# Window attention with a softplus feed-forward: one head's attention weights scaled on ScalarE, the other's on VectorE

## Chip, core and metric

The kernel runs on one core of a Trainium2 chip. The metric is the device time of one execution in microseconds (us). One execution is taken with a hardware profiler; times of the others come from runs without it. Engines: PE is TensorE (PEld its weight loads), DVE is VectorE, ACT is ScalarE, POOL is GpSimd, SP issues the transfers.

## What is computed

Eight batches of eight heads, 576 positions of 64 values. Each position attends to itself and the 63 before it; the result of all heads (4608 tokens of 512 values) goes through a feed-forward network of width 2048 with a softplus between its two products.

```python
scores = scale * np.matmul(q, k.transpose(0, 1, 3, 2))
mask = (rel >= 0) & (rel < window)          # rel = row - column, window = 64
scores = np.where(mask, scores, -1000000000.0)
attn = np.exp(scores - np.max(scores, axis=-1, keepdims=True))
attn = attn / (np.sum(attn, axis=-1, keepdims=True) + 1e-09)
out = np.matmul(attn, v)
...
h = x @ w_in
g = np.maximum(h, 0.0) + np.log1p(np.exp(-np.abs(h)))
return (g @ w_out).astype(np.float32)
```

## The kernel before

The tokens are cut into 12 blocks of 384 (`TB`), each of three tiles of 128 rows (`NJ`). For each block, `attention(g, hp)` runs four times, once for each pair of heads (`hp`), and the feed-forward runs 16 steps, one for each slice of 128 of the inner width. A step has `ffn_up` (12 products L450 into `ps_h`, then the softplus: absolute value L454, exponential L455 and logarithm L456 on ScalarE, the sum L458 on VectorE, and the split of the result in a high and a low part `g`, L460 and L461) and `ffn_down` (nine products L471 into `ps_o`). Products of full precision are made of three products of split operands. The order on TensorE puts the down-projection of a step behind the up-projection of the next.

One attention group has, for each of its three tiles j and for both heads `hh`: scores (L331 or L334), mask and minimum on VectorE (L342), the exponential with row sums on ScalarE (L345), then the sum plus 1e-9 (L352), its reciprocal (L353), and the scaling of the weights `p_t` by that reciprocal (L358), in place in SBUF. `p_t[0]` holds the first head, `p_t[1]` the second. Then each head's weights are transposed by TensorE (L379, L380), copied out of PSUM (L383, or L385 and L386), multiplied with the values (L416 or L427) and joined into `x` (L421, L422, or L431, L432 and L139, L140). For the first two blocks (`by_pe`) q and k are transposed by TensorE, and the scaling comes once behind all three tiles: six instructions in a row. For the others they are transposed by transfers (`tr<-nat`), and the scaling comes tile by tile.

In the opening, some 200 us, the kernel also loads the weights: 32 pieces of 512 KB of 64-bit numbers arrive by SP's queue (L156) and are put together into 32-bit numbers by `float64_split`: ScalarE (L161), GpSimd or VectorE (L162), VectorE (L163 to L165), ScalarE (L166) and GpSimd (L167).

The work is written as a list of events with due times (`BASE`, `PACE`, `STG`). A scheduler orders the instructions of each engine from it; TensorE's own order is kept as written from due time 100 on (`PE_ORDERED_FROM`). Each engine runs its instructions strictly in its order, and an instruction that waits holds all behind it.

Of the kernel before, what the change touches and what calls it, by code (L numbers as in the profile page):

```python
# [12 lines left out]
AF = mybir.ActivationFunctionType  # L13
ALU = mybir.AluOpType
# [22 lines left out]
def window_attention_softplus_ffn(  # L37
# [16 lines left out]
    nc = tc.nc  # L54
# [178 lines left out]
    def attention(g, hp):  # L233
# [6 lines left out]
        def bank():  # L240
            if not odd0:
                return ps_a.tile([P, 512], F32, name="ps_a")

            taken_ps[0] += 1
            return ps_o.tile([P, 512], F32, name=f"ps_o{taken_ps[0] % NJ}")
# [76 lines left out]
        rs = att.tile([P, NJ, 2], F32, name="rs", bufs=2)  # L322
        for j in range(NJ):
            first = j == 0 and not prev
            c0 = WIN if first else 0
            n = W - c0
            sp = bank()
            spv = sp[:, : 2 * n].rearrange("p (h c) -> p h c", h=2)
            kc = slice(j * P + WIN + c0, (j + 2) * P)
            if by_pe:  # L330
                mm(spv, qt[:, j * P : (j + 1) * P], kbd[:, :, j * P + c0 : j * P + W], start=True, stop=True)  # L331
            for hh in range(0 if by_pe else 2):
                for i, (a, b) in enumerate(((0, 0), (0, 1), (1, 0))):
                    mm(  # L334
                        spv[:, hh, :], tr_q[a][:, hh, j * P : (j + 1) * P], tr_k[b][:, hh, kc],
                        start=(hh == 0 and i == 0), stop=(hh == 1 and i == 2), skip_group_check=True,
                    )
            t = ORDER[g] * NJ + j
            m = mask_b if (t * P) % S + P > S else mask
            for hh in range(2):  # L340
                pv = p_t[hh][:, j, WIN + c0 :]
                nc.vector.tensor_tensor_reduce(  # L342
                    pv, spv[:, hh, :], m[:, c0:], 1.0, 3.0e38, ALU.add, ALU.min, mn[:, j, hh : hh + 1]
                )
                nc.scalar.activation(  # L345
                    pv, pv, AF.Exp, bias=mn[:, j, hh : hh + 1], scale=-1.0, accum_out=sm[:, j, hh : hh + 1]
                )
            if by_pe and j < NJ - 1:
                yield
                continue  # L350
            jr = slice(0, NJ) if by_pe else slice(j, j + 1)
            nc.vector.tensor_scalar(rs[:, jr, :], sm[:, jr, :], 1.0e-9, None, ALU.add)  # L352
            nc.vector.reciprocal(rs[:, jr, :], rs[:, jr, :])  # L353
            for jj in range(jr.start, jr.stop):
                for hh in range(2):
                    c0 = WIN if jj == 0 and not prev else 0
                    pv = p_t[hh][:, jj, WIN + c0 :]
                    nc.vector.tensor_scalar(pv, pv, rs[:, jj, hh : hh + 1], None, ALU.mult)  # L358
            yield


# [142 lines left out]
    for g in range(NB):  # L504
        for hp in range(NP):
            if g < 3:
                base = BASE[g] + PACE[g] * hp
            else:
                base = 2 * NF * (g - 1) + SHP * hp + SH
            stages = attention(g, hp)  # L510
            for at in STG if g >= 3 else STG2 if g >= 2 else STG0:
                events.append((base + at, lambda stages=stages: next(stages, None)))
# [44 lines left out]
```

## Time and profile before

| | |
|---|---|
| median of 3 runs | 1071.59 us (1070.12 to 1072.89) |
| the profiled execution | 1069.74 us, span 1067.9 us |
| busy: PE, PEld | 1028.4 us (96%), 924.3 us (87%) |
| busy: DVE, ACT, POOL | 789.0 us (74%), 650.0 us (61%), 224.7 us (21%) |
| scaling L358 | 288 instructions, 110.4 us |
| exponential L345 | 288 instructions, 127.0 us |

The span runs from the first to the last instruction. Busy shares are over the whole span, and say little of a stage with another limit; so the rows below are mostly of stretches of time. Where an engine is said to have been idle "<- X", X is the instruction whose end let it go on.

### The profile page before, as it was taken

How to read it: one execution, taken by the hardware profiler on the slowest of the kernel's cores; microseconds unless marked ns; L12 is line 12 of the kernel's file. 1: busy time of each engine (PE TensorE's matmuls, PEld its weight loads, DVE VectorE, ACT ScalarE, POOL GpSimd, SP SyncE). 2: the span in 40 equal slices, each digit the busy share in tenths (PEclk: the TensorE clock that was granted, in tenths of full speed). 3: DMA queues.
4: the chain of work that ended last, by engine and by line, in shares of the span. 5: the costliest groups of instructions: out<-in, count | busy, mean ns of one | idle time of the engine just before them, and what ended most of it. 6: DMA issues, size and time to landing. Idle time of an engine off the chain costs nothing.

```text
span 1067.9 us, 18172 instructions
## 1 busy us (share of the span) xinstructions
PE 1028.4 (96%) x6096; PEld 924.3 (87%) x6096; DVE 789.0 (74%) x2319; ACT 650.0 (61%) x1669; POOL 224.7 (21%) x217
## 2 busy tenths in 40 slices
PE   7797988999999999999999999999999999999998
PEld 5576867888999899999999999999999999999996
DVE  4999899866777777777777777777777777865433
ACT  6786666666665666566656666656666665655333
POOL 4354355631111111112111111111211111110000
PEclk9999998999999999999999999999999999999999
DMA  7754645255334434343344334424434533520000
GB/s 197 198 140 105 169 105 146 67 127 119 70 71 101 96 79 105 64 97 81 81 96 96 84 76 93 107 60 88 102 74 84 115 80 62 131 51 1 30 1 30
DMA packets 296222, 98.20 MB, mean 92 GB/s; under 512 B 280512, under 2 KB 288704, under 8 KB 296128
## 3 DMA queue, kind: packets, MB, share of 16 engines
q1 hardware_dynamic: 296128, 97.03, 40.0%
q8 instruction: 48, 0.79, 0.3%
q14 instruction: 46, 0.38, 0.1%
HBM read 50.07 MB, written 10.22 MB: 56 GB/s over the span
## 4 chain that ended last, share of the span: by engine, by line
PE 78%; DVE 12%; DMA 4%; ACT 3%; issue 2%; SPq 1%; POOL 0%; DVEq 0%; ACTq 0%
PE ps_h L450 32%; PE ps_o L471 31%; PE ps_a L334 5%; PE ps_a L427 4%; PE ps_a L380 2%; DMA tr<-nat 2%; PE ps_a L379 2%; DVE p_t L358 2%; DVE osb L165 2%; DVE osb L164 1%; DVE osb L162 1%; DVE p_t L342 1%; DVE osb L163 1%; SPq L198 1%; DVE u L458 1%
## 5 line engine op out<-in xcount | busy, mean ns | idle before, releaser
L450 PE MATMUL ps_h<-x,w 128*128 128x384 f32 x2304 | 458.4, 344 | 15.4 <-DVE u L458 11.8
L471 PE MATMUL ps_o<-w,g 128*128 128x512 f32 x1728 | 438.7, 397 | 6.3 <-ACT g L460 4.3
L450 PEld LDWEIGHTS ps_h<-x,w 128*128 128x128 f32 x2304 | 400.6, 189 | 27.5 <-DVE u L458 12.5
L471 PEld LDWEIGHTS ps_o<-w,g 128*128 128x128 f32 x1728 | 318.1, 188 | 65.6 <-ACT g L460 4.6
L458 DVE SCALAR_TENSOR_TENSOR u<-ps_h,u 128x384 f32<-128x384 f32 x192 | 106.0, 552 | 139.7 <-ACT u L456 139.5
L454 ACT ACTIVATE u<-ps_h 128x384 f32<-128x384 f32 x192 | 93.6, 488 | 179.4 <-PE ps_h L450 177.2
L345 ACT ACTIVATE p_t<-p_t,mn 128x192 f32<-128x192 f32 (+1 forms) x288 | 127.0, 443 | 63.5 <-DVE mn L342 63.2
L140 POOL TENSOR_TENSOR x<-xf,x 128x384 fp32r<-128x384 f32 x40 | 41.1, 1027 | 460.6 <-DVE rs L352 362.9
L358 DVE TENSOR_SCALAR p_t<-p_t,rs 128x192 f32<-128x192 f32 (+1 forms) x288 | 110.4, 429 | 2.9
L342 DVE CUSTOM_DVE_ANT_0 p_t<-ps_a,mask 128x192 f32<-128x192 f32 (+1 forms) x244 | 77.3, 343 | 46.5 <-PE ps_a L334 36.1
L455 ACT ACTIVATE u<-u 128x384 f32<-128x384 f32 x192 | 100.7, 526 | 4.1
L456 ACT ACTIVATE u<-u 128x384 f32<-128x384 f32 x192 | 100.6, 524 | 3.2
L461 DVE TENSOR_TENSOR g<-u,g 128x384 fp32r<-128x384 f32 x160 | 89.5, 559 | 3.8 <-DVE g L460 0.5
L385 ACT CAST pt<-ps_a 128x512 fp32r<-128x512 f32 (+1 forms) x144 | 59.0, 417 | 33.7 <-PE ps_a L380 21.9
L312 POOL TENSOR_TENSOR nat<-q_in,nat 128x384 bf16<-128x384 f32 x40 | 38.6, 965 | 187.8 <-ACT nat L311 152.1
L386 DVE TENSOR_TENSOR pt<-ps_a,pt 128x512 fp32r<-128x512 f32 (+1 forms) x144 | 67.9, 477 | 12.3 <-ACT pt L385 10.7
L334 PE MATMUL ps_a<-tr 128*128 128x192 bf16 (+1 forms) x720 | 74.8, 246 | 0.9 <-DVE xf L432 0.7
L460 DVE CAST g<-u 128x384 fp32r<-128x384 f32 x176 | 67.9, 386 | 5.9
L380 PE MATMUL ps_a<-ident,p_t 128*128 128x128 f32 x276 | 66.6, 276 | 1.4 <-DVE p_t L358 1.3
L427 PEld LDWEIGHTS ps_a<-pt,vt 128*128 128x128 f32 (+1 forms) x608 | 64.0, 163 | 3.9 <-issue 0.5
L427 PE MATMUL ps_a<-pt,vt 128*128 128x64 f32 (+4 forms) x608 | 64.5, 247 | 0.4 <-DVE mn L342 0.4
L431 ACT COPY xf<-ps_a 64x384 f32<-64x384 f32 x80 | 38.1, 477 | 40.3 <-PE ps_a L427 37.5
(91 smaller groups left out, 1019.3 us busy)
## 6 DMA issues: line engine op xcount, KB each, us to landing
out_dram<-raw SPq DMA_DIRECT2D x12, 512.0 KB, 3.2
q_in<-in_q_dram SPq DMA_DIRECT2D x56, 96.0 KB, 2.6
raw<-in_moe_w_in_dram SPq DMA_DIRECT2D x10, 512.0 KB, 4.2
raw<-in_moe_w_out_dram SPq DMA_DIRECT2D x10, 512.0 KB, 4.2
k_in<-in_k_dram SPq DMA_DIRECT2D x32, 128.0 KB, 3.5
v_in<-in_v_dram SPq DMA_DIRECT2D x32, 128.0 KB, 2.8
raws<-in_moe_w_in_dram SPq DMA_DIRECT2D x6, 512.0 KB, 4.2
raws<-in_moe_w_out_dram SPq DMA_DIRECT2D x6, 512.0 KB, 5.0
```

Source lines behind the costliest of these rows:

```text
L334: mm(spv[:, hh, :], tr_q[a][:, hh, j * P : (j + 1) * P], tr_k[b][:, hh, kc], start=(hh == 0 and i == 0), stop=(hh == 1 and i == 2), skip_g ...
L342: nc.vector.tensor_tensor_reduce(pv, spv[:, hh, :], m[:, c0:], 1.0, 3.0e38, ALU.add, ALU.min, mn[:, j, hh : hh + 1])
L345: nc.scalar.activation(pv, pv, AF.Exp, bias=mn[:, j, hh : hh + 1], scale=-1.0, accum_out=sm[:, j, hh : hh + 1])
L358: nc.vector.tensor_scalar(pv, pv, rs[:, jj, hh : hh + 1], None, ALU.mult)
L427: mm(av[: D if lo else P, osl], vt[:, vb, hh, : 1 if lo else 2, :], pt[hh][lo][:, psl], start=(i == 0), stop=(i == len(order) - 1), skip_g ...
L450: mm(hv, weight(0, a, f)[:, c * P : (c + 1) * P], x[b][c], start=(i_mm == 0), stop=(i_mm == 3 * NC - 1))
L454: nc.scalar.activation(u, hv, AF.Abs)
L455: nc.scalar.activation(u, u, AF.Exp, scale=-1.0)
L456: nc.scalar.activation(u, u, AF.Ln, bias=1.0)
L458: nc.vector.scalar_tensor_tensor(gf, hv, 0.0, u, ALU.max, ALU.add)
L461: (nc.vector if g >= 2 else nc.gpsimd).tensor_tensor(gt[1], gf, gt[0].bitcast(F32), ALU.subtract)
L471: mm(ops[g][j], gt[a][:, js], weight(1, b, f), start=(first and i == 0), stop=(last and i == 2),)
```

## The change

Of the two heads of a group, the first is scaled on VectorE as before, the second by an ACTIVATE (Copy, with the reciprocal as a per-partition scale) on ScalarE. That moves 144 of the 288 instructions. Lines behind it have numbers higher by 3: the scaling on VectorE is L361, that on ScalarE L359, the reciprocal still L353, and the softplus L457, L458, L459 (ScalarE) and L461 (VectorE).

```diff
                 for hh in range(2):
                     c0 = WIN if jj == 0 and not prev else 0
                     pv = p_t[hh][:, jj, WIN + c0 :]
-                    nc.vector.tensor_scalar(pv, pv, rs[:, jj, hh : hh + 1], None, ALU.mult)
+                    if hh:
+                        nc.scalar.activation(pv, pv, AF.Copy, scale=rs[:, jj, hh : hh + 1])
+                    else:
+                        nc.vector.tensor_scalar(pv, pv, rs[:, jj, hh : hh + 1], None, ALU.mult)
             yield
```

VectorE's order, in the opening, at the first group of the second block (the run of six that starts at 47.85 us in the trace of before); `p_t_101` is the first head, `p_t_102` the second, `osb` a weight piece on its way. Before:

```order
L352 TENSOR_SCALAR rs<-sm 128x6
L164 SCALAR_TENSOR_TENSOR osb<-raws,osb 128x512
L353 RECIPROCAL rs<-rs 128x6
L165 SCALAR_TENSOR_TENSOR osb<-raws,osb 128x512
L358 TENSOR_SCALAR p_t_101<-p_t_101,rs 128x128
L358 TENSOR_SCALAR p_t_102<-p_t_102,rs 128x128
L358 TENSOR_SCALAR p_t_101<-p_t_101,rs 128x192
L358 TENSOR_SCALAR p_t_102<-p_t_102,rs 128x192
```

And now:

```order
L352 TENSOR_SCALAR rs<-sm 128x6
L165 SCALAR_TENSOR_TENSOR osb<-raws,osb 128x512
L353 RECIPROCAL rs<-rs 128x6
L425 TENSOR_TENSOR x_3_0_407<-ps_o_408,x_3_0_406 128x384
L361 TENSOR_SCALAR p_t_101<-p_t_101,rs 128x128
L361 TENSOR_SCALAR p_t_101<-p_t_101,rs 128x192 x2
L162 TENSOR_SCALAR osb<-osb 128x512
```

Three scalings stand there instead of six, and the next weight step follows at once; the join of `x` (L422, now L425), which stood behind the six, comes ahead of the three.

ScalarE's order for the same group, from its last two exponentials to the first softplus steps. Before:

```order
L345 ACTIVATE p_t_102,sm<-p_t_102,mn 128x192
L293 COPY kbd_114<-ps_a 64x384 x2
L166 CAST w_109<-osb 128x512
L421 CAST x_3_0_406<-ps_o_408 128x384
L282 ACTIVATE qpt<-ps_a 128x384
L166 CAST w_111<-osb 128x512
L161 ACTIVATE osb<-raw 128x512
```

And now:

```order
L345 ACTIVATE p_t_102,sm<-p_t_102,mn 128x192
L424 CAST x_3_0_406<-ps_o_408 128x384
L282 ACTIVATE qpt<-ps_a 128x384
L293 COPY kbd_114<-ps_a 64x384 x2
L161 ACTIVATE osb<-raw 128x512
L166 CAST w_111<-osb 128x512
L359 ACTIVATE p_t_102<-p_t_102,rs 128x128
L359 ACTIVATE p_t_102<-p_t_102,rs 128x192 x2
L457 ACTIVATE u<-ps_h 128x384 x2
```

The three scalings of the second head stand behind the weight cast and ahead of the softplus.

ScalarE's order in the long stretch behind the opening, at the third tile of an attention group (30 of the 40 groups behind the third block look like this). Before:

```order
L345 ACTIVATE p_t_101,sm<-p_t_101,mn 128x192
L345 ACTIVATE p_t_102,sm<-p_t_102,mn 128x192
L454 ACTIVATE u<-ps_h 128x384
L455 ACTIVATE u<-u 128x384
L456 ACTIVATE u<-u 128x384
L385 CAST pt_5289<-ps_a 128x64
```

And now:

```order
L345 ACTIVATE p_t_101,sm<-p_t_101,mn 128x192
L345 ACTIVATE p_t_102,sm<-p_t_102,mn 128x192
L457 ACTIVATE u<-ps_h 128x384
L458 ACTIVATE u<-u 128x384
L359 ACTIVATE p_t_102<-p_t_102,rs 128x192
L459 ACTIVATE u<-u 128x384
L388 CAST pt_5289<-ps_a 128x64
```

The scaling came in between the exponential and the logarithm of a feed-forward step. The scalings of the other two tiles stand ahead of the absolute value of the step before.

## Rows read from the trace of the kernel before

**Rows 1.** Busy time by engine in stretches, start:end, length, then granted clock.

```profile
core 0: us, PE busy (x) PEld busy (x) DVE busy (x) ACT busy (x) POOL busy (x), PEclk, DMA share, GB/s
25.00:205.00 180.00, 154.48 (x821) 129.21 (x819) 171.39 (x406) 121.89 (x309) 88.73 (x68) 0.96 0.53 138
300.00:1000.00 700.00, 699.33 (x4312) 642.36 (x4311) 516.05 (x1612) 427.89 (x1110) 101.08 (x104) 1.00 0.39 83
...
25.00:100.00 75.00, 61.46 (x311) 48.77 (x309) 74.10 (x189) 57.62 (x157) 34.17 (x27) 0.96 0.61 160
100.00:150.00 50.00, 44.84 (x260) 38.91 (x260) 44.84 (x98) 31.40 (x75) 23.38 (x19) 1.00 0.39 108
150.00:205.00 55.00, 48.18 (x254) 41.52 (x252) 52.45 (x121) 32.88 (x78) 31.18 (x24) 0.94 0.54 136
...
8.00:22.00 14.00, 11.13 (x54) 7.73 (x54) 8.64 (x44) 10.04 (x34) 2.46 (x5) 1.00 0.88 247
```

**Rows 2.** The same by stretches, of the scaling L358 alone (VectorE).

```profile
25.00:100.00 75.00, 15.39 (x32) 0.96 0.61 160
100.00:150.00 50.00, 5.75 (x12) 1.00 0.39 108
150.00:205.00 55.00, 8.05 (x14) 0.94 0.54 136
```

**Rows 3.** Groups, 25 to 205 us: count | busy us, mean ns | idle before, releasers.

```profile
L450 PE MATMUL ps_h<-x,w 128*128 128x384 f32 x300 | 66.4, 359 | 14.6 <-DVE u L458 11.1 <-ACT x L421 2.3 <-POOL w L167 0.9
...
L358 DVE TENSOR_SCALAR p_t<-p_t,rs 128x192 f32<-128x192 f32 (+1 forms) x56 | 29.2, 577 | 0.2
```

**Rows 4.** Order of time, VectorE then GpSimd: start, length, instructions [idle before].

```profile
14.71 1.40 DVE L358 TENSOR_SCALAR p_t<-p_t,rs 128x128 f32<-128x128 f32 x6
...
47.85 3.44 DVE L358 TENSOR_SCALAR p_t<-p_t,rs 128x128 f32<-128x128 f32 x6
...
19.80 1.49 POOL L162 TENSOR_SCALAR osb<-osb 128x512 f32<-128x512 f32 x1 [10.70 <-ACT osb L161]
...
47.77 2.71 POOL L167 TENSOR_TENSOR w<-osb,w 128x512 fp32r<-128x512 f32 x2 [6.09 <-ACT w L166]
```

**Rows 5.** Order of time at 59 us: last exponential of a group, then its reciprocal.

```profile
58.81 0.46 ACT L345 ACTIVATE p_t<-p_t,mn 128x192 f32<-128x192 f32 x1
59.16 0.20 ACT L345 ACTIVATION_READ_ACCUMULATOR p_t<-p_t,mn 128x1 f32 x1
...
60.29 0.19 DVE L353 RECIPROCAL rs<-rs 128x6 f32<-128x6 f32 x1
```

**Rows 6.** Order of time at 598 us: ScalarE, VectorE, TensorE.

```profile
598.75 0.53 ACT L455 ACTIVATE u<-u 128x384 f32<-128x384 f32 x1
599.31 0.53 ACT L456 ACTIVATE u<-u 128x384 f32<-128x384 f32 x1
...
598.60 0.17 DVE L353 RECIPROCAL rs<-rs 128x2 f32<-128x2 f32 x1
...
601.03 0.56 DVE L461 TENSOR_TENSOR g<-u,g 128x384 fp32r<-128x384 f32 x1
...
602.71 2.23 PE L471 MATMUL ps_o<-w,g 128*128 128x512 f32 x9
```

**Rows 7.** Order of time at 497 us: ScalarE, VectorE, TensorE.

```profile
497.06 0.53 ACT L455 ACTIVATE u<-u 128x384 f32<-128x384 f32 x1
...
497.27 0.17 DVE L353 RECIPROCAL rs<-rs 128x2 f32<-128x2 f32 x1
...
499.73 0.55 DVE L461 TENSOR_TENSOR g<-u,g 128x384 fp32r<-128x384 f32 x1
...
500.38 2.25 PE L471 MATMUL ps_o<-w,g 128*128 128x512 f32 x9
```

## The prediction

> **What bounds the kernel now.** I read the stretches first, since a share over the whole span mixes stages with different limits. From 300 to 1000 us TensorE is busy 699.33 of 700 us at a granted clock of 1.00 (its 2.4 GHz level), while VectorE and ScalarE have idle time [rows 1]. There the end moves only if TensorE is made to wait. From 25 to 205 us it is different: VectorE is busy 171.39 of 180 us, TensorE 154.48, ScalarE 121.89, GpSimd 88.73 [rows 1]. So TensorE has 25.5 us of holes in the opening, and the row of the up-projection's products says who makes them: of 14.6 us of idle before them, 11.1 ended with VectorE's softplus sum (L458) [rows 3]. That sum waits its turn in VectorE's queue among the weight splits and the attention weights' scaling. Broken down, VectorE is busy 74.10 of 75 us from 25 to 100, 44.84 of 50 from 100 to 150, and 52.45 of 55 from 150 to 205 [rows 1]: no gaps worth the name in the first and last of these, 5.2 us of gaps in the middle one. My reading is that the opening is paced by VectorE's queue, and that from about 205 us on the time is TensorE's work. What the change is worth is how much sooner the opening ends.
>
> **What leaves VectorE.** Half of the 288 scalings, one head of two. In the opening the row shows 56 of them with 29.2 us, a mean of 0.577 us; by stretches 32, 12 and 14 (two are counted at a border) with 15.39, 5.75 and 8.05 us [rows 2, 3]. Half is 28: 16 + 6 + 6 after rounding. What one is worth on the queue lies between two rows. With GpSimd quiet, six of them take 1.40 us from start to end, 0.23 each [rows 4]. At 47.85 us six take 3.44 us, 0.57 each, and two GpSimd subtractions run from 47.77 for 2.71 us beside them [rows 4]. So the long ones are long because of GpSimd. Taken out, one saves at least 0.23 us, 28 x 0.23 = 6.4 us, and at most its mean, 28 x 0.52 = 14.6 us (29.2 / 2). Which it is depends on whether the blocked time goes with the instruction or passes to its neighbour in the queue. GpSimd's 88.73 us of work are the same in both kernels. In the contended run, 2.0 us of delay (3.44 - 1.40) met 2.71 us of GpSimd: with three instructions instead of six, part of the delay would fall on the step behind, which is often another slow one, part on a step that isn't slowed. I take 0.35 us, nearer to the quiet row, since the queue behind is full: 28 x 0.35 = 9.8 us.
>
> A rule speaks for the lower end. The Trainium skill, SBUF — State Buffer, in its part on the two sides of the memory, says that VectorE's two-port instructions and GpSimd share a port pair as an exclusive lock for a whole instruction, and ScalarE has its own ports. That agrees with the two rows on the runs of six; by it the wait passes to the next two-port instruction, and the sum would be made with 0.23. That result is the first rival below.
>
> **What of it reaches the end.** In the two stretches without gaps, 22 instructions leave: 22 x 0.35 = 7.7 us. In the middle one VectorE already waits 5.2 us for others, so I count its 6 at nothing; counted fully they would add 2.1. The weight splits, the scalings that stay and the softplus sums stand in about the same mix in the new order, so the same work is pulled forward and no long step goes in ahead of it.
>
> **What comes onto ScalarE.** 144 scalings of 128x192 (some of 128x128). The trace has no plain scaling of that size there; the nearest is the exponential of the same tile with a per-partition operand: 0.46 us, and its accumulator read starts 0.35 us after it [rows 5]. So 0.35 to 0.46 us each: bounds for 28 of them are 9.8 and 12.9 us, onto an engine that has 58 us of idle time in the opening. Covered by that idle time, it costs nothing; if the cover is gone it costs those 9.8 to 12.9 us. Less than nothing it can't be: ScalarE drops no work. The first 25 us are the exception: between 8 and 22 us ScalarE is busy 10.04 of 14 us and VectorE 8.64 [rows 1], so neither has a full queue, and the chain runs from one to the other. Six scalings come to ScalarE there, ahead of the second pair's exponentials, and six quiet ones of 0.23 leave VectorE: between -1.4 (all the VectorE time is saved, ScalarE hidden) and +2.1 us (6 x 0.35, nothing saved). I take +1.2, two thirds of the way up, since the exponentials that follow in ScalarE's queue gate the next scaling. Sum: -7.7 + 1.2 = -6.5 us. The lower bound of the gain is 22 x 0.23 - 2.1 = 3.0 us, the upper 14.6 + 1.4 = 16.0.
>
> **The new wait.** The scaling on ScalarE waits for VectorE's reciprocal, and stands at the head of an in-order queue. Behind it stand, in the opening, the weight casts (L166), the absolute values (L161) and the first softplus steps; TensorE and GpSimd wait for those. In the stretch bound by TensorE, the order shows for 30 of the 40 attention groups the third scaling between the softplus's exponential and its logarithm. At 598 us that reciprocal ends at 598.77, the exponential at 599.28: the scaling finds its operand ready and pushes the logarithm from 599.31 by about 0.35 us. The split of g (L461) would end 0.35 later than 601.59, and TensorE starts the down-projection at 602.71 [rows 6]. So this is covered by 1.1 us of slack. In five groups the scaling stands ahead of the exponential. At 497 us the reciprocal ends at 497.44, the exponential had begun at 497.06: a push of some 0.75 us. There L461 ends at 500.28 and TensorE starts at 500.38 [rows 7]; its low part is read by the third product, two products later (2 x 0.23 us, nine taking 2.1), so such a place can cost 0.2 us. Two such places: under 0.5 us, left out of the sum. The transposes of the second head come a step after those of the first, so they are not hit.
>
> The Trainium skill, ScalarE: Activation LUTs, section Rules for kernel authors, says to put multiplications on VectorE and not on ScalarE. Per instruction this case's rows agree (0.23 us quiet against an estimated 0.35 to 0.46); the sum, made on the queue that is full, goes the other way, and by the rule alone the opening would lose 28 x 0.12 = 3.4 us.
>
> **Rivals.** (1) The blocked time stays: each removed scaling saves only the quiet 0.23, so 22 x 0.23 = 5.1, less 1.2, gives -3.9 us. For it: GpSimd's work doesn't change. Against: many VectorE steps in between read from TensorE's results and are not seen to slow down. (2) The relief is hidden anyway: the weights' transfers or ScalarE become the pace of the opening as soon as VectorE is quicker, and the end stays within 2 us either way. For it: the 5.2 us of gaps in the middle. Against: the queue that is full over 130 of 180 us. (3) Slower: ScalarE's queue is held at the new scalings. At 60 us the last exponential's read ends at 59.36 and the reciprocal at 60.48 [rows 5], 1.1 us. The opening has 18 such groups (five of three, thirteen single). Each held 1.1 us, with 28 x 0.35 of work, makes 30 us on ScalarE. It has 58 idle, but these are not where the holds fall; if about half, 16 us, lies on the path, the result is 16 - 9.8 = +6 us. It decides from the point where more than a third of the 30 us isn't covered. Against it: in the new order one to five other instructions stand between the exponentials and the scaling, which run in that time. (4) Slower in the long stretch: the scaling costs some 1.5 us instead of 0.4, or the reciprocal comes late, and 40 places each lose 0.3 us past the slack: +12 - 6.5 = +5.5 us. Against: 1.1 us of slack in the row.
>
> **How the numbers follow.** The profiled execution took 1069.74 us, 1.84 more than its span of 1067.9; the median of the runs is 1071.59, 1.85 above that execution. With -6.5: 1063.2 for an execution like the profiled one, 1065.1 for the median. Rivals in the median: (1) 1067.7, (2) 1071.6, (3) 1077.6, (4) 1077.1. Chances: the forecast 0.50, (1) 0.18, (2) 0.16, (3) 0.12, (4) 0.04. A measurement of this kernel tells about 0.3%, 3.2 us, from no change. The forecast and two thirds of (1) lie beyond that: 0.62 faster; (2) and the rest of (1): 0.22; slower 0.16. The range runs from the forecast's upper bound of the gain, 1071.6 - 16.0 = 1055.6, to 1073.5, which takes in nearly all of (2) and leaves out (3) and (4).
>
> **What would show it.** In the profile after: VectorE's busy time from 25 to 205 us down by 8 to 14 us; the last weight split (L165) and the first gapless stretch of TensorE earlier by some 6 us, and the same distance kept up to the end; TensorE's idle time before the up-projection less than 14.6 us; 144 scalings on ScalarE of 0.40 to 0.46 us each, some 60 us in all. 300 to 1000 us should stay gapless on TensorE. If the remaining scalings average over 0.6 us in the opening and the other VectorE steps grow, rival (1) holds. If ScalarE's idle time before L359 is long, and TensorE's waits name ScalarE (L166, L421 and its followers) instead of L458, it is (3). The prediction is wrong as a whole if the opening ends no earlier although VectorE's busy time fell, or if waits of TensorE appear after 300 us.

## The result, and the profile after

The changed kernel takes 1073.24 us (median of 20 runs, 1070.83 to 1075.73); the kernel before in the same comparison 1071.41 (20 runs, 1068.98 to 1072.89). The ratio is 1.0019, with a 95% interval of 1.0011 to 1.0027: some 2 us slower, less than the 0.3% that the prediction named as telling a change from none. The forecast was 1065.1. The time lies inside the forecast's range (1055.6 to 1073.5), but at its slow end, which was put there for rival 2. The profiled execution took 1072.42 us, its span 1070.6 (before 1067.9).

From the page of the profile, busy time by engine, then the two scalings (idle before, releaser):

```profile
PE 1029.3 (96%) x6096; PEld 928.6 (87%) x6096; DVE 756.2 (71%) x2175; ACT 702.4 (66%) x1813; POOL 224.9 (21%) x217
...
L359 ACT ACTIVATE p_t<-p_t,rs 128x192 f32<-128x192 f32 (+1 forms) x144 | 62.3, 444 | 27.5 <-DVE rs L353 24.3
...
L361 DVE TENSOR_SCALAR p_t<-p_t,rs 128x192 f32<-128x192 f32 (+1 forms) x144 | 67.3, 477 | 3.0
```

The edit does what it says: VectorE has 33 us less over the span, ScalarE 52 more. The stretches of [rows 1], now:

```profile
core 0: us, PE busy (x) PEld busy (x) DVE busy (x) ACT busy (x) POOL busy (x), PEclk, DMA share, GB/s
25.00:205.00 180.00, 153.66 (x810) 131.72 (x809) 165.84 (x380) 132.14 (x340) 88.96 (x68) 0.94 0.53 138
300.00:1000.00 700.00, 699.54 (x4308) 641.55 (x4307) 493.55 (x1519) 465.76 (x1216) 101.12 (x104) 1.00 0.39 82
25.00:100.00 75.00, 62.15 (x322) 51.96 (x320) 72.27 (x176) 63.79 (x174) 35.45 (x27) 0.95 0.60 158
100.00:150.00 50.00, 43.14 (x238) 37.58 (x239) 41.84 (x97) 32.01 (x80) 24.90 (x18) 0.97 0.42 118
150.00:205.00 55.00, 48.38 (x252) 42.19 (x251) 51.73 (x110) 36.34 (x88) 28.62 (x23) 0.91 0.52 127
```

The long stretch is as gapless as before: 699.54 of 700 us on TensorE. The opening isn't shorter: from 25 to 205 us VectorE's busy time fell by 5.5 us, and TensorE shows 11 matmuls and 0.8 us of busy time less than before. The products of the up-projection, the row of [rows 3] from 25 to 205 us:

```profile
L453 PE MATMUL ps_h<-x,w 128*128 128x384 f32 x294 | 68.3, 372 | 13.5 <-DVE u L461 8.6 <-DVE x L425 3.5 <-ACT x L424 1.4
```

The wait for the softplus sum shrank from 11.1 to 8.6, and a wait for VectorE's join of `x` (L425) took its place. So VectorE was relieved, and TensorE got nothing of it. The prediction's own sign of being wrong as a whole stands here: VectorE's busy time fell, and the opening ends no earlier. One place shows how. VectorE from 49 to 57 us in the changed kernel, in order of time: start, length, instruction; behind it ScalarE's two logarithms, whose results the two sums L461 wait for:

```profile
49.10 0.42 DVE L162 TENSOR_SCALAR osb<-osb 128x512 f32<-128x512 f32 x1
49.55 0.43 DVE L163 TENSOR_SCALAR osb<-osb 128x512 uint32<-128x512 uint32 x1
50.01 0.69 DVE L164 SCALAR_TENSOR_TENSOR osb<-raw,osb 128x512 uint32<-128x512 uint32 x1
...
51.55 0.69 DVE L165 SCALAR_TENSOR_TENSOR osb<-raw,osb 128x512 uint32<-128x512 uint32 x1
...
52.75 0.42 DVE L162 TENSOR_SCALAR osb<-osb 128x512 f32<-128x512 f32 x1
53.20 0.43 DVE L163 TENSOR_SCALAR osb<-osb 128x512 uint32<-128x512 uint32 x1
53.66 1.81 DVE L164 SCALAR_TENSOR_TENSOR osb<-raw,osb 128x512 uint32<-128x512 uint32 x1
55.40 0.34 DVE L342 CUSTOM_DVE_ANT_0 p_t<-ps_a,mask 128x192 f32<-128x192 f32 x1
...
55.95 0.68 DVE L165 SCALAR_TENSOR_TENSOR osb<-raw,osb 128x512 uint32<-128x512 uint32 x1
56.55 0.54 DVE L461 SCALAR_TENSOR_TENSOR u<-ps_h,u 128x384 f32<-128x384 f32 x1
...
53.45 0.95 ACT L459 ACTIVATE u<-u 128x384 f32<-128x384 f32 x2
```

Both logarithms are done at 54.40; the first sum starts at 56.55. Two whole weight pieces (L162 to L165) stand ahead of it, the last steps of them ahead of minima that ScalarE waits for (L342 at 55.40, behind a step that took 1.81 us where its like at 50.01 took 0.69). The first and the third sum in the kernel before, then the third in the changed one:

```profile
56.40 0.55 DVE L458 SCALAR_TENSOR_TENSOR u<-ps_h,u 128x384 f32<-128x384 f32 x1
...
67.61 0.55 DVE L458 SCALAR_TENSOR_TENSOR u<-ps_h,u 128x384 f32<-128x384 f32 x1
...
70.90 0.54 DVE L461 SCALAR_TENSOR_TENSOR u<-ps_h,u 128x384 f32<-128x384 f32 x1
```

So the first sum gained nothing, the third came 3.3 us late, and the last one of the kernel 2.67 us. The last weight split (L165) starts earlier, at 198.60 against 200.98, others up to 8.6 us earlier. The time that VectorE gained went to weight pieces, not to feed-forward steps.

### The profile page after: what moved, and what is told of

Same layout as the page of the kernel before. It is cut to its first block, busy times and chain, and to the rows that moved or that the text cites. A ratio compares the mean times of both kernels' runs of the same rounds, so it can differ in the third digit from the quotient of the medians.

```text
span 1070.6 us, 18257 instructions
## 1 busy us (share of the span) xinstructions
PE 1029.3 (96%) x6096; PEld 928.6 (87%) x6096; DVE 756.2 (71%) x2175; ACT 702.4 (66%) x1813; POOL 224.9 (21%) x217
## 4 chain that ended last, share of the span: by engine, by line
PE 81%; DVE 9%; DMA 3%; ACT 3%; issue 2%; SPq 1%; POOL 1%; DVEq 0%; ACTq 0%; POOLq 0%
PE ps_h L453 33%; PE ps_o L474 33%; PE ps_a L334 5%; PE ps_a L430 4%; PE ps_a L383 2%; PE ps_a L382 2%; DMA tr<-nat 2%; DVE osb L164 1%; DVE osb L165 1%; DMA raw<-in_moe_w_in_dram 1%; DVE u L461 1%; DVE p_t L342 1%; DVE osb L163 1%; DVE osb L162 1%; ACT p_t L345 1%
## 5 line engine op out<-in xcount | busy, mean ns | idle before, releaser
L461 DVE SCALAR_TENSOR_TENSOR u<-ps_h,u 128x384 f32<-128x384 f32 x192 | 106.4, 554 | 170.5 <-ACT u L459 170.3
L457 ACT ACTIVATE u<-ps_h 128x384 f32<-128x384 f32 x192 | 93.6, 488 | 124.1 <-PE ps_h L453 122.8
L342 DVE CUSTOM_DVE_ANT_0 p_t<-ps_a,mask 128x192 f32<-128x192 f32 (+1 forms) x244 | 77.3, 344 | 44.6 <-PE ps_a L334 33.8
L458 ACT ACTIVATE u<-u 128x384 f32<-128x384 f32 x192 | 100.8, 525 | 3.8
L459 ACT ACTIVATE u<-u 128x384 f32<-128x384 f32 x192 | 99.9, 521 | 2.1
L464 DVE TENSOR_TENSOR g<-u,g 128x384 fp32r<-128x384 f32 x160 | 90.4, 565 | 3.9 <-DVE g L463 0.5
L359 ACT ACTIVATE p_t<-p_t,rs 128x192 f32<-128x192 f32 (+1 forms) x144 | 62.3, 444 | 27.5 <-DVE rs L353 24.3
L334 PE MATMUL ps_a<-tr 128*128 128x192 bf16 (+1 forms) x720 | 74.3, 246 | 1.3 <-DVE pt L389 1.2
L361 DVE TENSOR_SCALAR p_t<-p_t,rs 128x192 f32<-128x192 f32 (+1 forms) x144 | 67.3, 477 | 3.0
```

The lines of the kernel that those rows point to most:

```text
L334: mm(spv[:, hh, :], tr_q[a][:, hh, j * P : (j + 1) * P], tr_k[b][:, hh, kc], start=(hh == 0 and i == 0), stop=(hh == 1 and i == 2), skip_g ...
L342: nc.vector.tensor_tensor_reduce(pv, spv[:, hh, :], m[:, c0:], 1.0, 3.0e38, ALU.add, ALU.min, mn[:, j, hh : hh + 1])
L457: nc.scalar.activation(u, hv, AF.Abs)
L458: nc.scalar.activation(u, u, AF.Exp, scale=-1.0)
L459: nc.scalar.activation(u, u, AF.Ln, bias=1.0)
L461: nc.vector.scalar_tensor_tensor(gf, hv, 0.0, u, ALU.max, ALU.add)
```

## Experiments

Two things had changed at once: the engine of 144 instructions, and the order that the scheduler made of everything else (of some 6,700 TensorE instructions 475 stood elsewhere, of VectorE's 190). To part them, the first two kernels hold each engine to a given order: a table of instruction numbers, and an order-only dependency from each to the one before it in the table, with no semaphore and no wait. A moved scaling gets the place in the program that its counterpart had.

```diff
+def lock_order(tc):
...
+    for n in seq:
+        i = here.get(f"I-{n}")
...
+        if e in last:
+            tc.add_manual_dep(
+                i, last[e], mybir.DependencyInfo(mybir.DependencyClass.NoSync, mybir.DependencyReason.DATA),
+                reason="lock",
+            )
+        last[e] = i.name
...
         for at, emit in events:
             if at >= PE_ORDERED_FROM:
                 emit()
+    lock_order(tc)
```

**Edit in the old order, and new order without the edit.** The first is the changed kernel with the table of the kernel before, the second the kernel before with the table of the changed one.

> The changed kernel (second head's scaling on ScalarE), but every engine's instructions held in the order of the kernel before; a moved scaling stands in ScalarE's queue at the place in the program where VectorE's scaling stood. This separates the change of engine from the new order that the scheduler made of it. Theory A (the relief is real, as I forecast, and the new order ate it): about 6 us faster than before, 1064 to 1067 us, the softplus sums of the opening earlier by 4 to 7 us from 60 us on. Theory B (the relief never was there: GpSimd's blocked time passes to the other VectorE steps and what is left is hidden): within 1.5 us of before, 1070 to 1073 us, VectorE busy from 25 to 205 us some 6 us less than 171.39. Theory C (the ScalarE work is what costs: holds and pushes in ScalarE's queue): slower than before by 2 us or more, 1073 to 1077 us, with TensorE waits on ScalarE's L424, L166 or L457 grown.

Measured: 1066.21 us against 1070.97, ratio 0.9954 (0.9939 to 0.9969): 4.9 us faster. The softplus sums of the opening come 1.4 to 4.3 us earlier from 60 us on, not 4 to 7.

> The converse: both heads scaled on VectorE as before, but every engine held in the order of the changed kernel, each scaling of the second head in VectorE's queue where ScalarE's stood. Theory A (relief real, order ate it): the order alone costs some 8 us, 1077 to 1081 us. Theory B (relief nothing, order costs 2 us): 1073 to 1075 us, about as the changed kernel. Theory C (ScalarE's work costs, order is neutral): 1070 to 1072 us, as before.

Measured: 1077.39 us, ratio 1.0063 (1.0045 to 1.0082): 6.7 us slower. So theory A: the relief is real, and the new order costs more than it brings. The edit's worth is the same in both orders: 0.9954 in the old one, 1.0019 / 1.0063 = 0.9956 in the new one. The sum of both, -4.9 + 6.7, is the changed kernel's +2. In the traces of these two runs TensorE and VectorE run in the order that each was given.

The same place in the run with the edit in the old order, VectorE, then the logarithms:

```profile
49.90 0.41 DVE L163 TENSOR_SCALAR osb<-osb 128x512 uint32<-128x512 uint32 x1
50.45 0.43 DVE L162 TENSOR_SCALAR osb<-osb 128x512 f32<-128x512 f32 x1
50.79 0.68 DVE L164 SCALAR_TENSOR_TENSOR osb<-raw,osb 128x512 uint32<-128x512 uint32 x1
51.39 0.42 DVE L163 TENSOR_SCALAR osb<-osb 128x512 uint32<-128x512 uint32 x1
51.73 0.35 DVE L342 CUSTOM_DVE_ANT_0 p_t<-ps_a,mask 128x192 f32<-128x192 f32 x1
...
52.28 0.69 DVE L165 SCALAR_TENSOR_TENSOR osb<-raw,osb 128x512 uint32<-128x512 uint32 x1
52.88 0.69 DVE L164 SCALAR_TENSOR_TENSOR osb<-raw,osb 128x512 uint32<-128x512 uint32 x1
53.49 0.55 DVE L461 SCALAR_TENSOR_TENSOR u<-ps_h,u 128x384 f32<-128x384 f32 x1
...
52.26 0.53 ACT L459 ACTIVATE u<-u 128x384 f32<-128x384 f32 x1
...
53.47 0.55 ACT L459 ACTIVATE u<-u 128x384 f32<-128x384 f32 x1
```

Here the two pieces are interleaved with the minima, the last split (L165) of the second waits behind the sum, and the sum starts 0.70 us behind its logarithm, at 53.49, 3.1 us ahead of the changed kernel (0.6 of them were there ahead of the first scaling).

**Only the opening, only the long stretch** (planned anew).

```diff
-                    if hh:
+                    if hh and g < 3:
```

> Second head's scaling on ScalarE for the first three blocks only (the opening and some groups behind it), as before for the nine others; ordered anew by the scheduler. All theories put nearly the whole +2 us into the opening: 1072.5 to 1074 us. If the long stretch were what costs, this would be at 1071 us or below.

Measured: 1072.28 us, ratio 1.0018 (1.0007 to 1.0029), 0.2 us under what was expected. The other half has `g >= 3`:

> The second head's scaling on ScalarE only from the fourth block on; the first three blocks as before. From the two traces the long stretch adds 0.4 us: 1071.5 to 1072 us by all theories. If it were to lose what rival 4 of the prediction says (a late reciprocal or a push past the slack in 36 groups), it would be 1073 us or more, and the opening would be cleared.

Measured: 1071.05 us, ratio 1.0008 (0.9998 to 1.0017). In the traces, TensorE and VectorE run the opening of the first kernel in the changed kernel's order, and that of the second in the order of before, so these two plans part the stretches cleanly. The opening alone gives the whole result; the long stretch is at most 1.8 us, and can't be told from nothing.

**Old and new order by parts in time** (both with the edit). The table follows one order up to the fourth softplus sum, about 80 us, which is entry 600 of the old and 612 of the new; then come the entries that are left, in the other order:

```python
table = old[:600] + [n for n in new if n not in old[:600]]
table = new[:612] + [n for n in old if n not in new[:612]]
```

> The changed kernel, held in the order of the kernel before up to the fourth softplus sum (about 80 us) on every engine, and in the new order from there on. Theory A1 (the new order loses its 6 to 7 us at the start: in the trace of the changed kernel the third softplus sum already stands 6.2 us behind that of the run with the old order): 1065 to 1068 us. Theory A2 (the loss comes from what follows, the weight pieces put ahead of softplus sums between 80 and 200 us): 1071 to 1074 us. Half and half: 1068 to 1071 us.

Measured: 1071.05 us, ratio 1.0008 (0.9999 to 1.0016).

> The counterpart: the changed kernel in the new order up to the fourth softplus sum, in the order of the kernel before from there on. Theory A1 (loss at the start): 1071 to 1074 us, as the changed kernel. Theory A2 (loss behind 80 us): 1065 to 1068 us.

Measured: 1069.40 us, ratio 0.9988 (0.9975 to 1.0001). Neither A1 nor A2: beside the edit in the old order, the new order costs 3.6 us in the first 80 us and 5.8 behind them, and both together some 7. The parts don't add up, since a splice of two orders is a third one; and the 12 runs of the second spread from 1065.3 to 1072.8. In the trace of the second, the delay is there by the first sum (57.30 against 53.49, of which 1.4 us stand ahead of the first scaling) and is 3.5 us from 205 us to the end.

**One engine in the old order, the others planned anew.** The table is cut to the instructions of TensorE, then to those of VectorE:

```python
table = [n for n in old if engine[n] == "PE"]
table = [n for n in old if engine[n] == "DVE"]
```

> The changed kernel with TensorE alone held in the order of the kernel before, the other engines ordered anew by the scheduler. If it is TensorE's new order in the first part (value products and down-projections in larger runs behind one wait, with a clock at half speed after it) that loses the time: 1065 to 1068 us. If it is the order of VectorE's queue (weight pieces ahead of softplus sums, scalings of one head only): 1071 to 1075 us.

Measured: 1074.24 us, ratio 1.0035 (1.0023 to 1.0047).

> The changed kernel with VectorE alone held in the order of the kernel before, the others ordered anew. If VectorE's new order is what loses the time: 1065 to 1068 us. If TensorE's or ScalarE's new order does: 1071 to 1075 us. If the orders only lose together (one engine's order fits the others'), both this and the run with TensorE's old order lie between 1067 and 1072 us.

Measured: 1075.10 us, ratio 1.0044 (1.0032 to 1.0056). Holding one engine to the old order brings nothing back: the second run is slower than the changed kernel, the first can't be told from it. That doesn't clear either engine's order, since the engines left free were planned anew around the one that was held, and so are in yet another order.

**The same work, planned anew.** Not the edit; only the loop over the heads in the scaling of the kernel before runs backwards:

```diff
-                for hh in range(2):
+                for hh in (1, 0):
```

> The kernel before with the same instructions on the same engines; only the loop over the two heads of the scaling runs backwards (second head first), and the scheduler plans anew from that. Theory R (what the changed kernel lost in the new order is what this kernel loses by any new plan, since the order of before is a good one among several): 1073 to 1078 us. Theory S (the loss is special to the scaling on ScalarE, as the scheduler reacts to VectorE's relief): 1069 to 1072 us, as before.

Measured: 1075.69 us, ratio 1.0053 (1.0037 to 1.0069): 5.7 us slower. Theory R. An exchange of neighbours that moves no work from one engine to another changes TensorE's order in more places than the edit did, and costs about what the edit's new order costs.

**Relief alone, ScalarE's work alone, twice the dose** (all in the order of the kernel before). The first leaves out the second head's scaling, and its result lacks it.

```diff
-                    if hh:
-                        nc.scalar.activation(pv, pv, AF.Copy, scale=rs[:, jj, hh : hh + 1])
-                    else:
+                    if not hh:
```

> The scaling of the second head is left out altogether (no instruction for it on any engine, so the result lacks that scaling); all else in the order of the kernel before. This is the relief of VectorE without ScalarE's new work. With the prediction's +1.2 us for ScalarE's part: 1.2 us faster than the run with the edit in the old order, 1064 to 1065.5 us. If ScalarE's part costs nothing: the same as that run, 1065.5 to 1067 us. If ScalarE's part eats half of the relief: 1060 to 1062 us.

Measured: 1066.46 us, ratio 0.9959 (0.9944 to 0.9975), 4.4 us faster.

```diff
+    scr = cpool.tile([P, W], F32, name="scr")
+    nc.gpsimd.memset(scr, 0.0)
...
                     nc.vector.tensor_scalar(pv, pv, rs[:, jj, hh : hh + 1], None, ALU.mult)
+                    if hh:
+                        nc.scalar.activation(scr[:, : W - c0], scr[:, : W - c0], AF.Copy, scale=rs[:, jj, hh : hh + 1])
```

> The kernel before in its own order (VectorE scales both heads), and ScalarE beside it does the 144 scalings once more on a scratch tile of the same size, with the same reciprocals as scale, at the places where they stand in the run with the edit in the old order; nobody waits for the scratch. This is ScalarE's new work and its wait for the reciprocal without VectorE's relief. With the prediction's +1.2 us: 1071.5 to 1073 us. If ScalarE's work is covered: 1069.5 to 1071.5 us. If the held queue costs what rival 3 says: 1075 us or more.

Measured: 1070.46 us, ratio 0.9999 (0.9988 to 1.0010). The two agree: with the work left out the kernel is no faster than with it on ScalarE, and the work added to ScalarE costs nothing. One scaling's worth of ScalarE per pair is covered. The second run shows as well that holding the order costs nothing by itself.

```diff
-                    if hh:
-                        nc.scalar.activation(pv, pv, AF.Copy, scale=rs[:, jj, hh : hh + 1])
-                    else:
-                        nc.vector.tensor_scalar(pv, pv, rs[:, jj, hh : hh + 1], None, ALU.mult)
+                    nc.scalar.activation(pv, pv, AF.Copy, scale=rs[:, jj, hh : hh + 1])
```

> Both heads' scalings on ScalarE (288 instead of 144), every engine in the order of the kernel before: twice the dose. If VectorE's queue paces the opening throughout and ScalarE's work is covered, twice the gain of the run with one head: 1060 to 1063 us. If the gain saturates, because another engine or the transfers become the pace: 1064 to 1067 us. If ScalarE's queue becomes the pace: 1068 us or more.

Measured: 1072.23 us, ratio 1.0012 (1.0002 to 1.0022): not twice the gain but all of it lost, 6 us behind one head. The waits of VectorE from 8 to 55 us (waited for, us in total, times, longest), with both heads on ScalarE:

```profile
DVE x L422 <- ACT x L421: 5.1, 2, 4.2
```

And with one:

```profile
DVE x L425 <- ACT x L424: 2.2, 1, 2.2
```

Before it was 0.3. In the first 23 us ScalarE runs all six scalings of the first group among the exponentials of the second, then those of the second group; its copy of `x` comes late, and VectorE stands idle. Counted from the first minimum of the second group (L342), which stands ahead of every scaling, the first weight split comes 2.5 us later than before, with one head 0.4 later. So ScalarE becomes the pace there, by its work and not by rival 3's hold: it waits 0.5 us for a reciprocal in that stretch. Where the rest of the 6 us is lost was not located.

**The weight steps at the other order's places** (both with the edit). The steps of L156 to L167 are taken out of one order and put in where as many of the other steps stand ahead of them as in the other order:

```python
table = place(rest=new without weights, weights=old)
table = place(rest=old without weights, weights=new)
```

> The changed kernel in its own new order, but all steps of the weight loading (L156 to L167, on SP, ScalarE, GpSimd and VectorE) at the places among the others that they have in the order of the kernel before. Theory W (the new order loses its 6.9 us because weight pieces run earlier, ahead of softplus sums and minima in VectorE's queue): 1065.5 to 1068.5 us. Theory N (it is the order of the attention and feed-forward steps among themselves): 1071 to 1075 us. Theory M (no one part: orders fit or don't fit as a whole, so a mixture is worse than either): 1074 us or more.

Measured: 1079.32 us, ratio 1.0081 (1.0067 to 1.0095).

> The converse: the edit in the order of the kernel before, with the weight loading's steps at the places that they have in the new order. Theory W: 1071 to 1075 us. Theory N: 1065.5 to 1068.5 us. Theory M: 1074 us or more here too.

Measured: 1075.02 us, ratio 1.0045 (1.0032 to 1.0059). Theory M. In the old order, moving the weight steps alone costs 9.7 us; but putting them back in the new order doesn't help, it costs 6.6 more than the changed kernel. So it isn't the weight steps' places in themselves that cost: either mixture is worse than both orders. The stretch from 25 to 100 us with the edit in the old order:

```profile
25.00:100.00 75.00, 63.27 (x332) 51.73 (x331) 70.93 (x177) 64.35 (x176) 35.47 (x28) 0.95 0.61 160
```

The same with the weight steps moved:

```profile
25.00:100.00 75.00, 61.60 (x303) 50.31 (x302) 66.60 (x170) 60.93 (x167) 34.47 (x26) 0.92 0.58 156
```

With the weights moved, every engine is busy for less time: each waits for another in turn. VectorE loses 4.3 us of busy time in 75.

**A third block with both heads on ScalarE, and the heads exchanged.** In the old order:

```diff
-                    if hh:
+                    if hh or g == 2:
```

> The edit in the order of the kernel before, and in the third block (g equal to 2, whose 12 pairs of scalings run between 110 and 205 us) the first head's scaling on ScalarE too. In the run with both heads there the distance to before shrank by 2.2 us in that stretch, though it had lost 3.5 us at 14 to 20 us. If that is VectorE's relief in the stretch: 1063 to 1065 us, the best so far. If it is only idle time that catches up: 1065.5 to 1067 us, as with one head.

Measured: 1063.49 us (1063.46 to 1064.33) against 1070.31, ratio 0.9939 (0.9927 to 0.9952): 6.5 us faster, the lowest time of all, and what was expected if it is VectorE's relief in that stretch. It is 1.6 us beyond one head alone, with intervals that overlap. From 150 to 205 us:

```profile
150.00:205.00 55.00, 48.09 (x270) 41.72 (x269) 51.41 (x113) 40.31 (x100) 29.36 (x23) 0.97 0.50 124
```

TensorE gets 270 matmuls done there; with one head on ScalarE in the old order it was 259, and before 254 [rows 1].

Planned anew, with the first head on ScalarE:

```diff
-                    if hh:
+                    if not hh:
```

> The edit with the heads exchanged (first head on ScalarE, second on VectorE), planned anew by the scheduler: the same work on each engine as in the changed kernel in yet another order. If the time of a new plan is a matter of where it happens to fall (three plans so far cost 5.7 to 6.9 us beside the order of before): anywhere from 1068 to 1076 us, and not equal to the changed kernel's 1073. If the loss belongs to the division of the work between the engines: 1072 to 1074 us, as the changed kernel.

Measured: 1079.31 us, ratio 1.0084 (1.0071 to 1.0098). The same work on each engine as in the changed kernel, and by the ratios 7 us slower, outside both expectations. So the division of the work alone doesn't set the time. How much of the 7 us is the plan and how much the choice of the head (the first one is transposed first) is not parted, since this kernel was not run in a held order.

## Why the prediction was wrong

**The step that failed** is the last sentence of the part on what reaches the end: that the weight splits, scalings and sums stand in about the same mix in the new order, so that the same work is pulled forward and no long step goes in ahead of it. I read the new order at three places and took the rest to be alike. It isn't: the order alone costs 6.7 us, and at 53 us the long step stands ahead of the sum. Without that cost the sum would have been near: -4.9 measured against -6.5. In part that is luck: the terms below are off, and not all of the 4.9 is found in the trace.

**No rival held this.** All four priced the edit, none the plan. The second, relief hidden anyway, named 1071.6, nearest to the result, but for a reason that fell: relief reached the end in both orders. With the order held, rival 1 does as well as the forecast: its -3.9 lies inside the interval, and its sign is there (the scalings that stay average 0.67 us, and other steps grew).

**What bounds the kernel**: right. From 300 to 1000 us TensorE is gapless in every order shown, and what the opening won or lost stayed to the end (in the trace with the old order 3.25 us at the last weight split, 3.78 at the last sum).

**The saving of one scaling**, taken as 0.35 between 0.23 and 0.52, can be read from the run in the old order. Between the starts of the first and the last weight split (L165), VectorE's busy time, in the kernel before:

```profile
23.51:200.98 177.47, 169.40 (x407) 0.96 0.54 141
```

And with the edit in the old order:

```profile
22.67:197.73 175.06, 161.66 (x380) 0.95 0.55 143
```

7.74 us less for 27 scalings: 0.29 each, nearer to the quiet row than I took it. The scalings themselves fell by 11.3 us, from 27.85 to 16.59; the other 3.5 came back as longer steps beside them. The scalings that stayed got longer too, a mean of 666 ns from 25 to 201 us:

```profile
L361 DVE TENSOR_SCALAR p_t<-p_t,rs 128x192 f32<-128x192 f32 (+1 forms) x28 | 17.7, 666 | 0.2
```

Before, the mean over both heads was 577 [rows 3], and over the first head alone 596. So of some 14 us that the 27 took, half of 27.85, about 6 passed on, to other steps and to the scalings that stayed. GpSimd is what they meet: scalings of the first head from 25 to 205 us with no GpSimd instruction beside them have a mean of 0.31 us in all three traces, those with one 0.81 before, 0.90 with the edit in the old order and 0.62 in the changed kernel; the softplus sums, which read TensorE's result, have 0.55 either way.

The Trainium skill, SBUF — State Buffer, in its part on the two sides of the memory, says that of VectorE's two-port instructions and GpSimd's, the one that starts first holds the shared port pair for its whole instruction and the other blocks. The traces agree (0.31 us quiet, 0.62 to 0.90 beside GpSimd), and rival 1 was right that blocked time stays: about 6 of 14 us passed on. In the changed kernel's own order it passes to other rows, L163 with 22.7 us against 19.8 from 25 to 205 us, and L310 on `k_in` with 5.6 against 3.4, while the scalings there average 462 ns.

**The share that reaches the end**, all of it in two stretches without gaps, was too high. Between the same two marks VectorE's idle time rose from 8.07 to 13.40 us, so 2.4 of the 7.7 us came through. From the first to the fifteenth split, before and with the edit in the old order:

```profile
23.51:97.79 74.28, 73.41 (x190) 0.97 0.61 159
...
22.67:94.35 71.68, 67.65 (x175) 0.97 0.63 166
```

Here 2.60 us came through, while 0.87 us of idle time grew to 4.03; behind it nothing did (the rest took 103.19 us before, 103.38 with the edit). A queue without gaps shows that it is full, not that it alone sets the pace: as soon as it was quicker, it waited more for ScalarE (L309, 1.7 us in the first part, where it waited none before), for TensorE (L334, 1.6 us behind it against 0.7) and for GpSimd (L464, 0.9).

**The first 25 us** were taken as +1.2, between -1.4 and +2.1. The first split came 0.84 us earlier, but that isn't the edit's doing. 1.20 us are there ahead of every moved instruction, at the first minimum of the second group, behind TensorE's first scores. Before, then with the edit in the old order:

```profile
6.76 3.75 PE L331 MATMUL ps_a<-kbd,qpt 128*128 128x256 f32 x6
13.46 0.29 DVE L342 CUSTOM_DVE_ANT_0 p_t<-ps_o,mask 128x128 f32<-128x128 f32 x1 [2.26 <-PE ps_o L331]
...
6.84 2.77 PE L331 MATMUL ps_a<-kbd,qpt 128*128 128x256 f32 x6 [0.24 <-ACT kbd L293]
12.26 0.29 DVE L342 CUSTOM_DVE_ANT_0 p_t<-ps_o,mask 128x128 f32<-128x128 f32 x1 [1.97 <-PE ps_o L331]
```

Six traces have the same order up to that point (the kernel before, the edit in the old order, that order up to 80 us, the scaling left out, both heads, the third block), and this minimum starts anywhere from 12.26 to 13.46 us in them, so the 1.20 us come from the executions and not from the edit. From it to the first split it takes 10.05 us before, and 10.41, 9.55 and 10.73 in the three that scale one head on ScalarE there (the edit in the old order, that order up to 80 us, the third block): an effect of -0.5 to +0.7 us, neither the +1.2 nor a gain. The -3.79 us between the two profiled executions are then -1.20 ahead of the edit, +0.36 to the first split, -2.41 to the last and -0.54 behind it. The runs say -4.9, with an interval of -6.5 to -3.3; the traces show 2.6 of it behind the first minimum, and where the rest arises is not shown.

**ScalarE** was right: 28 scalings in the opening at a mean of 436 ns, inside the bounds of 0.35 to 0.46, hidden. Held at the reciprocal it was for 3.8 us in the opening; rival 3 had 18 x 1.1, some 20 us. The rule in the Trainium skill, ScalarE: Activation LUTs, Rules for kernel authors, to keep multiplications off ScalarE, doesn't decide here: with the order held, moving them there gains 4.9 us, with twice as many it loses it again.

**The new wait in the long stretch** was right too. The prediction prices two of the five groups where the scaling stands ahead of the exponential; five of them at 0.2 us would be 1.0. Neither is seen: TensorE's idle time from 300 to 1000 us is 0.46 us in all. At 601 us the scaling stands between exponential and logarithm as the order showed; rows of ScalarE, then the split of g, then TensorE's down-projection, beside [rows 6]:

```profile
601.49 0.53 ACT L458 ACTIVATE u<-u 128x384 f32<-128x384 f32 x1
601.93 0.44 ACT L359 ACTIVATE p_t<-p_t,rs 128x192 f32<-128x192 f32 x1
602.27 0.51 ACT L459 ACTIVATE u<-u 128x384 f32<-128x384 f32 x1
...
603.80 0.56 DVE L464 TENSOR_TENSOR g<-u,g 128x384 fp32r<-128x384 f32 x1
...
605.24 1.09 PE L474 MATMUL ps_o<-w,g 128*128 128x512 f32 x4
```

The logarithm starts 0.25 us behind the exponential's end, and the split ends at 604.36, 0.9 us ahead of TensorE.

**What stays open**: which steps of the new order lose the time. One place is shown above; the parts in time lose both, single engines in the old order bring nothing back, and exchanging the places of the weight steps loses either way. No run changed the due times (`BASE`, `PACE`, `STG`), so whether the scheduler can be led to a plan that keeps the 4.9 us is open too.

A part of the loss is TensorE's clock. From 25 to 205 us the granted clock, which is 2.4 GHz at 1.00, was 0.96 before, 0.95 with the edit in the old order, 0.94 after and 0.92 with the weights moved in the old order. There TensorE was busy at the lower level, 1.2 GHz, for 12.2, 14.0, 19.4 and 26.0 us of these traces. In the changed kernel twelve products of the up-projection at 119 us, behind waits for VectorE, then the granted clock there, then twelve products at full clock:

```profile
118.72 3.91 PE L453 MATMUL ps_h<-x,w 128*128 128x384 f32 x12 [0.64 <-DVE u L461]
119.00:122.00 3.00, 3.00 (x11) 0.50 1.00 295
...
603.06 2.34 PE L453 MATMUL ps_h<-x,w 128*128 128x384 f32 x12
```

If half of the time at the lower level is lost, the clock makes 2.7 of the some 7 us between the two orders with the edit, and 6.0 of the 9.7 with the weights moved, and the rest is waiting. That is an estimate from one trace of each; no run parts the two.

## What to carry over

Where a scheduler makes the order, an edit is two changes, and the second can be the larger: here every new plan that the scheduler made of the opening cost 5.7 us or more, that of an exchange of neighbours too. Hold the order of the kernel before to learn what the edit is worth, and price "planned anew" as a rival of its own, by what an edit that is worth nothing does to the time. A full queue gives back only as much as the next one allows: of 7.7 us taken off it, 2.4 arrived, and with a second dose everywhere the gain was gone. And before a trace explains a difference, look whether it was there ahead of the edit: 1.2 us were here.

## What the runs showed that was not expected

The spread between plans of the same work: 1071 to 1077 us for the division of the work before, 1066 to 1079 for that of the changed kernel. VectorE's steps lengthened when neighbours left: a scaling of the first head had a mean of 596 ns before, 666 with the edit in the old order and 462 in the new, by how often GpSimd ran beside it and for how long. And 144 instructions of 0.44 us put onto ScalarE cost 0.1 us (ratio 0.9999, not to be told from nothing), while 144 more lost 6, although VectorE was relieved of them.
